# Twenty-eight of thirty-two attention steps put into a hardware loop of seven passes

## The chip, the cores and the metric

The kernel runs on one core of a Trainium2 chip. The core has five engines that run at the same time, each with an instruction queue of its own: TensorE (PE in the profile; its weight loads are listed as PEld), VectorE (DVE), ScalarE (ACT), GpSimd (POOL) and SyncE (SP). They order themselves by semaphores. Data come from memory through 16 DMA engines, which work through what the queues hand them; nearly every load here is issued by SyncE. The metric is the device time of one execution in microseconds (us).

## What is computed

A conditioned block decodes one token for each of 4 batch entries (B = 4): a layer norm with a condition-dependent scale and shift, attention over a cache of 4096 keys for 32 heads of width 128, and a small gated MLP. All tensors are bf16. The part that the change touches is the attention:

```python
q = (h @ wq).reshape(B, 1, 32, 128).transpose(0, 2, 1, 3)
scores = jnp.einsum('bhqd,bhkd->bhqk', q, k_cache) * 128 ** (-0.5)
p = softmax(scores, axis=-1)
o = jnp.einsum('bhqk,bhkd->bhqd', p, v_cache)
x = x + ga * (o.transpose(0, 2, 1, 3).reshape(B, 1, 4096) @ wo)
```

k_cache and v_cache have the shape (4, 32, 4096, 128), 134 MB each, and every element is used once.

## The kernel before

The attention is cut into 32 *quads*: quad i covers four heads, head group g = i // 4, of batch entry b = i % 4. The keys of one quad are 4 MB of contiguous memory and land in one SBUF tile of 128 partitions x 16384 elements (tag kt, two buffers that take turns); the values likewise (tag vt, two buffers, which the prologue uses first for the weights w_mod and wq).

The schedule is written by hand: each engine executes its instructions in the order in which the program emits them. The loop over the quads (line 429) is a Python loop, so all 32 steps are written out. Step i does this:

- SyncE: issue the load of K of quad i+1 (lines 92 and 431), at the first quad of a group also that group's slice wo_g of wo (line 436, 0.5 MB, two buffers), then the load of V of quad i (line 437). A load first waits until the last reader of its buffer is done.
- scores(i, half), lines 272 to 285, for the two halves of the keys: VectorE multiplies the K tile in place by the query (line 276, 128 x 8192 elements), and TensorE adds up the products over the head width with 16 matmuls against the identity (line 281) into a PSUM tile s_ps (two buffers). fold (line 290) reduces what is left over to S.
- softmax(i), lines 295 to 320: six short VectorE instructions, an exponential on ScalarE (line 311), then the probabilities P4 with a head mask (line 314; three buffers) and the row sums.
- values(i-1), lines 331 to 348: one matmul for the sum (zsum, line 327), 32 matmuls of P4 with V (line 341) into the PSUM tile big (two buffers), and a copy on ScalarE (line 347).
- diagonal(i-2) (line 354) and project(i-2) (lines 374 and 375) take the head outputs from there, divide and put them into oT; apply(i-2) (lines 381 to 408) multiplies a finished group's oT by wo_g into attn_ps, once for every four quads.

So work on a quad is spread over three steps: scores, one step later the values, one more step later the output. Quad 31 is special: its K comes in two pieces and its V in five, and behind them SyncE issues the weights that the end of the kernel needs (lines 440, 444, 446). The last V products are in values_last (line 363). Then comes the MLP, some 10 us of short instructions.

Small PSUM results (layer-norm sums, the outputs of the modulation, apply's transposition) use a PSUM tile with the tag small, one buffer.

Of the kernel before, what the change touches and what calls it, by code (L numbers as in the profile page):

```python
# [9 lines left out]
F32 = mybir.dt.float32  # L10
# [6 lines left out]
def kernel(  # L17
# [52 lines left out]
    def vslot(cols):  # L70
        return kvp.tile([P, cols], BF16, name="vt", bufs=2)

    wm = vslot(J * 6 * D)
# [3 lines left out]
    wq = vslot(J * G * GW)  # L77
# [3 lines left out]
    quads = [(g, b) for g in range(G) for b in range(B)]  # L81

    def kv_view(cache, i):
        g, b = quads[i]
        return cache[b, g * NH:(g + 1) * NH].rearrange("h (s n) d -> (h s) (n d)", s=R)

    def load(cache, i, tag, parts):
        t = kvp.tile([P, NT * DH], BF16, name=tag, bufs=2)
        a = 0
        for part in parts:  # L90
            b = a + NT * DH // part
            nc.sync.dma_start(out=t[:, a:b], in_=kv_view(cache, i)[:, a:b])  # L92
            a = b
        return t.rearrange("p (n d) -> p n d", d=DH)

    def load_k(i):
        return load(A_k_cache, i, "kt", (2, 2) if i == len(quads) - 1 else (1,))

    def load_v(i):
        return load(A_v_cache, i, "vt", (2, 4, 8, 16, 16) if i == len(quads) - 1 else (1,))  # L100

    NQ = len(quads)
# [23 lines left out]
    def keep_busy(n):  # L126

        if busy_ps[0] is None:
            busy_ps[0] = psum_s.tile([P, 4 * P], F32, name="big", bufs=2)
        for _ in range(n):  # L130
            nc.tensor.matmul(busy_ps[0], lhsT=ident, rhs=wide, start=True, stop=True)

    NB = 3
# [17 lines left out]
    def ln_stats(pool, psum, buf, ones, n, name, meanwhile=None):  # L151

        nc.vector.tensor_tensor(out=buf[:, 1], in0=buf[:, 0], in1=buf[:, 0], op=ALU.mult)
        ps = psum.tile([P, 2, n, B], F32, name="small", bufs=1)
# [38 lines left out]
    )  # L193

    def mod_part(oc):
        ps = psum_s.tile([P, J, B], F32, name="small", bufs=1)
        for jo in range(J):
            c0 = oc * D + (jo if oc < 2 else jo * P)
            cols = slice(c0, c0 + (P - 1) * J + 1, J) if oc < 2 else slice(c0, c0 + P)
            for j in range(J):  # L200
                nc.tensor.matmul(
                    ps[:, jo, :], lhsT=wm[:, j, cols],
                    rhs=sT[:, j, :], start=(j == 0), stop=(j == J - 1),
                )
        if oc in (1, 4):
            nc.vector.tensor_scalar_add(out=modT[:, oc], in0=ps, scalar1=1.0)
        else:
            nc.vector.tensor_copy(out=modT[:, oc], in_=ps)
# [13 lines left out]
    with tc.tile_pool(name="pre", bufs=1) as pre:  # L222
        xc_ps = psum_s.tile([P, J, 2 * B], F32, name="small", bufs=1)
# [5 lines left out]
        xt_ps = psum_s.tile([P, J, B], F32, name="big", bufs=2)  # L229
# [25 lines left out]
        wb_ps = psum_s.tile([P, 2], F32, name="small", bufs=1)  # L255
# [6 lines left out]
        for b in range(B):  # L262
            for g0 in range(0, G, 4):
                qp = psum_s.tile([P, 4, DH], F32, name="big", bufs=2)
                query(b, g0, 4, qp)
                nc.scalar.copy(out=qbc[:, b, g0:g0 + 4, :], in_=qp)


    with tc.tile_pool(name="psum_att", bufs=1, space=bass.MemoryType.PSUM) as psum:
        st = {}  # L270

        def scores(i, half):
            g, b = quads[i]
            kt = st["k", i][:, half * HT:(half + 1) * HT, :]
            q = qbc[:, b, g, :]
            nc.vector.tensor_tensor(  # L276
                out=kt, in0=kt, in1=q[:, None, :].to_broadcast([P, HT, DH]), op=ALU.mult,
            )
            ps = psum.tile([P, HT, DC], F32, name="s_ps", bufs=2)
            for cc in range(DH // DC):  # L280
                nc.tensor.matmul(  # L281
                    ps, lhsT=ident, rhs=kt[:, :, cc * DC:(cc + 1) * DC],
                    start=(cc == 0), stop=(cc == DH // DC - 1),
                )
            st["s", i, half] = ps

        def fold(i, half):
            if half == 0:
                st["S", i] = wk.tile([P, NT], F32, name="S", bufs=3)
            nc.vector.tensor_reduce(  # L290
                out=st["S", i][:, half * HT:(half + 1) * HT], in_=st.pop(("s", i, half)),
# [3 lines left out]
        def softmax(i):  # L295
            S = st.pop(("S", i))
            mx, P4 = mxs[i % NB], P4s[i % NB]
            nc.vector.tensor_reduce(out=mx[:, 0:1], in_=S, axis=AX.X, op=ALU.max)
            mT = wk.tile([P, R], F32, name="mT", bufs=2)
            nc.vector.transpose(out=mT, in_=mx)  # L300
            hm = wk.tile([P, 1], F32, name="hm", bufs=2)
            nc.vector.tensor_reduce(out=hm, in_=mT, axis=AX.X, op=ALU.max)
            hb = wk.tile([P, R], F32, name="hb", bufs=2)
# [3 lines left out]
            nm = wk.tile([P, R], F32, name="nm", bufs=2)  # L307
            nc.vector.transpose(out=nm, in_=hb)  # L308
            E = wk.tile([P, NT], F32, name="E", bufs=2)
            rs = wk.tile([P, 1], F32, name="rs", bufs=2)  # L310
# [7 lines left out]
            rs4 = wk.tile([P, NH], F32, name="rs4", bufs=3)  # L318
            nc.vector.tensor_scalar_mul(out=rs4, in0=mask4, scalar1=rs)
            st["rs4", i] = rs4  # L320

        def zsum(i):
            zo = psum.tile([P, 2, NH], F32, name="zo_ps", bufs=2)
            st["z", i], st["o", i] = zo[:, 0], zo[:, 1]
            if i == NQ - 1:
                st["z", i] = psum_s.tile([P, NH], F32, name="small", bufs=1)
            nc.tensor.matmul(
                st["z", i], lhsT=ones_f, rhs=st.pop(("rs4", i)), start=True, stop=True,
            )

        def values(i):


            P4 = P4s[i % NB]
            zsum(i)
            po = psum_s.tile([P, 4, DH], F32, name="big", bufs=2)
            NU = NT // 16
            for u in range(NU):
                for t in range(4):
                    n0 = 16 * u + 4 * t  # L340
                    nc.tensor.matmul(  # L341
                        po[32 * t:32 * t + 32], lhsT=P4[:, n0:n0 + 8, :],
                        rhs=st["v", i][:, n0:n0 + 4, :],
                        start=(u == 0), stop=(u == NU - 1), tile_position=(0, 32 * t),
                    )
            osb = wk.tile([P, 4, DH], F32, name="osb", bufs=2)
            nc.scalar.copy(out=osb, in_=po)  # L347
            st["osb", i] = osb

        def diagonal(i):  # L350

            osb = st.pop(("osb", i))
            for n in range(4):
                nc.tensor.matmul(  # L354
                    st["o", i], lhsT=osb[:, n, :], rhs=sel[:, NH * n:NH * n + NH],
                    start=(n == 0), stop=(n == 3),
                )

        def values_last(i):
            P4 = P4s[i % NB]  # L360
            zsum(i)
            for n in range(NT):
                nc.tensor.matmul(  # L363
                    st["o", i], lhsT=st["v", i][:, n, :], rhs=P4[:, n, :],
# [3 lines left out]
        def project(i):  # L368
            g, b = quads[i]
            if b == 0:  # L370
                st["oT", g] = wk.tile([P, NH, B], BF16, name="oT", bufs=2)
            oT = st["oT", g]
            rz = wk.tile([P, NH], F32, name="rz", bufs=2)
            nc.vector.reciprocal(out=rz, in_=st.pop(("z", i)))
            nc.vector.tensor_tensor(  # L375
                out=oT[:, :, b], in0=st.pop(("o", i)), in1=rz, op=ALU.mult,
            )
            if i == NQ - 1:
                apply(i)

        def apply(i):
            g, b = quads[i]
            if b == B - 1:
                oT = st.pop(("oT", g))
                if g < G - 1:
                    wo_g = st.pop(("wo", g))

                    pp = psum_s.tile([P, NH, B], F32, name="small", bufs=1)
                    for r in range(NH):
                        for hl in range(NH):  # L390
                            nc.tensor.matmul(
                                pp[hl * R:(hl + 1) * R, r, :], lhsT=ident[:, r::NH],
                                rhs=oT[:, hl, :], start=True, stop=True,
                                tile_position=(0, hl * R),
                            )
                    oT = wk.tile([P, NH, B], BF16, name="oP", bufs=2)
                    nc.vector.tensor_copy(out=oT, in_=pp)  # L397
                for hl in range(NH):
                    for jo in range(J):
                        nc.tensor.matmul(  # L400
                            attn_ps[:, jo, :],
                            lhsT=(wo_g[:, hl] if g < G - 1 else wo_l[hl // 2][:, hl % 2])[
                                :, jo * P:(jo + 1) * P],
                            rhs=oT[:, hl, :],
                            start=(g == 0 and hl == 0 and jo == 0),
                            stop=(g == G - 1 and hl == NH - 1),
                            skip_group_check=True,
                        )
# [18 lines left out]
        wo_l = [wk.tile([P, NH // 2, D], BF16, name=f"wo_l{a}", bufs=1) for a in range(2)]  # L427
        st["k", 0] = load_k(0)
        for i in range(NQ):
            if i + 1 < NQ:  # L430
                st["k", i + 1] = load_k(i + 1)
            if quads[i][1] == 0:
                g = quads[i][0]
                if g < G - 1:
                    st["wo", g] = wk.tile([P, NH, D], BF16, name="wo_g", bufs=2)
                    nc.sync.dma_start(out=st["wo", g], in_=wo_w[g])
            st["v", i] = load_v(i)
            if i == NQ - 1:
# [6 lines left out]
                for a, (j0, j1) in enumerate(JFS):  # L445
                    nc.sync.dma_start(out=wout[a], in_=wout_v[a])
            if i > 1:
# [3 lines left out]
            scores(i, 0)  # L451
            if i > 1:
                project(i - 2)
            scores(i, 1)
# [8 lines left out]
            if i > 1:  # L463
                apply(i - 2)
# [3 lines left out]
        project(NQ - 1)  # L468


    with tc.tile_pool(name="post", bufs=1) as post, \
# [67 lines left out]
        t_ps = psum_s.tile([J * B, P], F32, name="small", bufs=1)  # L539
# [36 lines left out]
```

## Time and profile before

| | |
|---|---|
| median of 3 runs | 667.62 us (667.53 to 667.81) |
| span of the profiled execution, first to last instruction | 665.5 us |
| read from memory | 282.73 MB, 425 GB/s over the span |
| longest busy engines | PE 415.7 us, DVE 402.6 us |
| K multiply, line 276 | 64 x 4.42 us |
| K sums on TensorE, line 281 | 1024 matmuls, 457 ns each in the mean |
| fold, line 290 | 64 x 0.69 us |
| K load, 4 MB, issue to landing | 26.0 us (median) |
| V load, 4 MB, issue to landing | 33.7 us (median) |
| SyncE's queue waiting for the multiply (line 276), for the K sums (line 281), for the V products (line 341) | 379.1, 139.5, 37.0 us |

The span and the runs' times are not the same thing: the profiled execution's own time, as the profile has it, is its span, and the runs' median lies 2.1 us above it, for what is done around the first and the last instruction.

The profile's views are read as follows. The page counts busy time of each engine, and shows it in 40 slices of the span as a digit for tenths. The DMA line is the share of the 16 DMA engines that is busy; q1 is SyncE's data queue, q8 and q14 bring instructions. The chain of waits is followed back from the last instruction: at each step it shows what released the instruction. SyncE's timeline lists the issue of each load. The trace also has a record for each DMA packet (start, length, bytes, queue) and for each landing: a load runs on 16 DMA engines, and each of them raises the load's semaphore when its part is in.

### The profile page before, as it was taken

The numbers are of one execution on the slowest core, as the hardware profiler recorded it, in microseconds if no ns is written. First come the engines' busy times: TensorE is split into PE (matmuls) and PEld (weight loads), VectorE is DVE, ScalarE is ACT, GpSimd is POOL, SyncE is SP. The second block draws the span as 40 slices with busy tenths as digits, with TensorE's granted clock in tenths as the row PEclk, the third lists the DMA queues.
The fourth block names the chain that finished last, engine by engine and source line by source line (L and its number), as shares of the span: only waits on it lengthen the run. The fifth ranks groups of instructions, "written<-read, shape, count | busy, mean of one in ns | idle before, by whom it ended". The sixth has DMA issues, their size and how long they took to land.

```text
span 665.5 us, 6939 instructions
## 1 busy us (share of the span) xinstructions
PE 415.7 (62%) x3024; PEld 204.6 (31%) x3024; DVE 402.6 (61%) x475; ACT 41.3 (6%) x115; POOL 4.7 (1%) x21
## 2 busy tenths in 40 slices
PE   2557776655677655676555477654657655657775
PEld 2223333222333322233222233232223322223334
DVE  2166776675556576547666456666555666655762
ACT  1200000000000000000000000000000000000002
POOL 2000000000000000000000000000000000000000
PEclk9977777668887667887667788676888766888795
DMA  9999999999999999999999999999999999999995
GB/s 379 439 425 427 437 439 424 429 438 434 427 428 441 428 428 434 435 426 434 433 436 424 436 435 430 423 439 435 428 431 435 433 430 432 437 426 435 428 417 236
DMA packets 12749, 283.17 MB, mean 426 GB/s; under 512 B 1448, under 2 KB 1968, under 8 KB 4016
## 3 DMA queue, kind: packets, MB, share of 16 engines
q1 hardware_dynamic: 12640, 282.73, 98.9%
q8 instruction: 23, 0.38, 0.2%
q14 instruction: 6, 0.05, 0.0%
q0 software_dynamic: 64, 0.00, 0.0%
q10 hardware_dynamic: 16, 0.01, 0.0%
HBM read 282.73 MB, written 0.00 MB: 425 GB/s over the span
## 4 chain that ended last, share of the span: by engine, by line
DMA 62%; PE 24%; DVE 12%; issue 0%; SPq 0%; ACT 0%; DVEq 0%
DMA kt<-in_A_k_cache_dram 58%; PE s_ps L281 24%; DVE kt L276 11%; DMA vt<-in_A_v_cache_dram 3%; DMA wout_437<-in_B_w_out_dram 1%; PE big L341 0%; DVE S L290 0%; ACT E L311 0%; SPq L92 0%; DVE P_1_109 L314 0%; DVE P_0_105 L314 0%; PE y_ps L522 0%; DVE nm L308 0%; DVE mT L300 0%; SPq L78 0%
## 5 line engine op out<-in xcount | busy, mean ns | idle before, releaser
L281 PE MATMUL s_ps<-kt,ident 128*128 128x512 bf16 x1024 | 293.5, 457 | 185.5 <-DVE kt L276 185.5
L276 DVE TENSOR_TENSOR kt<-kt,qbc 128x8192 bf16<-128x8192 bf16 x64 | 282.7, 4420 | 82.9 <-DMA kt<-in_A_k_cache_dram 82.9
L281 PEld LDWEIGHTS <-ident 128*128 128x128 bf16 x1024 | 116.4, 114 | 351.1 <-issue 229.8
L290 DVE TENSOR_REDUCE S<-s_ps 128x64 f32<-128x512 f32 x64 | 44.3, 692 | 125.5 <-PE s_ps L281 125.5
L354 PE MATMUL zo_ps<-sel,osb 128*128 128x4 f32 x248 | 33.2, 257 | 26.6 <-ACT osb L347 26.6
L311 ACT ACTIVATE E<-S,nm 128x128 f32<-128x128 f32 x32 | 12.8, 401 | 563.4 <-DVE nm L308 563.4
L354 PEld LDWEIGHTS zo_ps<-sel,osb 128*128 128x128 f32 x248 | 30.6, 194 | 38.4 <-ACT osb L347 38.4
L341 PE MATMUL big<-vt,P_0_105 128*32 128x512 bf16 x352 | 21.0, 380 | 1.5 <-DMA vt<-in_A_v_cache_dram 1.5
L341 PE MATMUL big<-vt,P_1_109 128*32 128x512 bf16 x320 | 19.1, 380 | 0.0
L341 PE MATMUL big<-vt,P_2_113 128*32 128x512 bf16 x320 | 19.1, 380 | 0.0
L347 ACT COPY osb<-big 128x512 f32<-128x512 f32 x31 | 17.6, 566 | 20.0 <-PE big L341 20.0
L215 PE MATMUL big<-vt,hbc 128*32 128x512 bf16 x128 | 9.6, 471 | 5.2 <-DMA vt<-in_A_wq_dram 5.2
L314 DVE TENSOR_TENSOR P_1_109<-E,mask_99 128x512 bf16<-128x512 f32 x11 | 7.6, 692 | 6.8 <-ACT E L311 6.8
L314 DVE TENSOR_TENSOR P_0_105<-E,mask_99 128x512 bf16<-128x512 f32 x11 | 7.6, 692 | 6.7 <-ACT E L311 6.7
L341 PEld LDWEIGHTS <-P_0_105 128*32 128x32 bf16 x352 | 8.4, 96 | 8.9 <-DMA vt<-in_A_v_cache_dram 1.6
L314 DVE TENSOR_TENSOR P_2_113<-E,mask_99 128x512 bf16<-128x512 f32 x10 | 6.9, 692 | 6.2 <-ACT E L311 6.2
L400 PE MATMUL attn_ps<-oP,wo_g 128*128 128x4 bf16 x112 | 3.8, 164 | 10.6 <-DVE oP L397 10.6
L341 PEld LDWEIGHTS <-P_1_109 128*32 128x32 bf16 x320 | 7.6, 96 | 6.7
L341 PEld LDWEIGHTS <-P_2_113 128*32 128x32 bf16 x320 | 7.6, 96 | 6.7
L375 DVE TENSOR_TENSOR oT<-zo_ps,rz 128x4 bf16<-128x4 f32 x32 | 5.4, 168 | 7.1 <-PE zo_ps L363 6.0
L215 PEld LDWEIGHTS <-hbc 128*32 128x32 bf16 x128 | 4.4, 114 | 10.3 <-issue 8.4
L308 DVE STREAM_TRANSPOSE nm<-hb 128x32 f32<-128x32 f32 x32 | 6.8, 212 | 1.1
(221 smaller groups left out, 131.1 us busy)
## 6 DMA issues: line engine op xcount, KB each, us to landing
kt<-in_A_k_cache_dram SPq DMA_DIRECT2D x31, 4096.0 KB, 26.0
vt<-in_A_v_cache_dram SPq DMA_DIRECT2D x31, 4096.0 KB, 33.7
vt<-in_A_wq_dram SPq DMA_DIRECT2D x1, 4096.0 KB, 20.4
kt<-in_A_k_cache_dram SPq DMA_DIRECT2D x2, 2048.0 KB, 24.8
wo_g<-in_A_wo_dram SPq DMA_DIRECT2D x7, 512.0 KB, 26.5
vt<-in_w_mod_dram SPq DMA_DIRECT2D x1, 3072.0 KB, 9.8
vt<-in_A_v_cache_dram SPq DMA_DIRECT2D x1, 2048.0 KB, 17.8
win_434<-in_B_w_in_dram SPq DMA_DIRECT2D x1, 1344.0 KB
```

The source lines that it names most:

```text
L215: nc.tensor.matmul(qp[hl * R:(hl + 1) * R, 0:n], lhsT=hbc[:, j, b, :], rhs=wv[:, g0:g0 + n, hl, :], start=(j == 0), stop=(j == J - 1), til ...
L276: nc.vector.tensor_tensor(out=kt, in0=kt, in1=q[:, None, :].to_broadcast([P, HT, DH]), op=ALU.mult,)
L281: nc.tensor.matmul(ps, lhsT=ident, rhs=kt[:, :, cc * DC:(cc + 1) * DC], start=(cc == 0), stop=(cc == DH // DC - 1),)
L290: nc.vector.tensor_reduce(out=st["S", i][:, half * HT:(half + 1) * HT], in_=st.pop(("s", i, half)), axis=AX.X, op=ALU.add,)
L308: nc.vector.transpose(out=nm, in_=hb)
L311: nc.scalar.activation(out=E, in_=S, func=AF.Exp, bias=nm[:, 0:1], scale=att_scale, accum_out=rs,)
L314: nc.vector.tensor_tensor(out=P4[:, 0:NT, :], in0=E[:, :, None].to_broadcast([P, NT, NH]), in1=mask4[:, None, :].to_broadcast([P, NT, NH]) ...
L341: nc.tensor.matmul(po[32 * t:32 * t + 32], lhsT=P4[:, n0:n0 + 8, :], rhs=st["v", i][:, n0:n0 + 4, :], start=(u == 0), stop=(u == NU - 1), ...
L347: nc.scalar.copy(out=osb, in_=po)
L354: nc.tensor.matmul(st["o", i], lhsT=osb[:, n, :], rhs=sel[:, NH * n:NH * n + NH], start=(n == 0), stop=(n == 3),)
L375: nc.vector.tensor_tensor(out=oT[:, :, b], in0=st.pop(("o", i)), in1=rz, op=ALU.mult,)
L400: nc.tensor.matmul(attn_ps[:, jo, :], lhsT=(wo_g[:, hl] if g < G - 1 else wo_l[hl // 2][:, hl % 2])[:, jo * P:(jo + 1) * P], rhs=oT[:, hl, :],
```

## The change

Quads 2 to 29 are no longer written out; they are four steps in a hardware loop of seven passes. Each engine runs the four steps and branches back. Steps 0, 1, 30 and 31 stay written out before and behind the loop. To make the four steps the same in each pass:

- every tile that was taken from a rotating pool becomes a fixed pair, picked by i % 2 (kt, vt, s_ps, zo_ps, S, E, rs, rs4, osb, big, P4, mx), or a single one (mT, hm, hb, nm, rz, oT, oP, wo_g). P4, mx, S and rs4 thereby go from three buffers to two, wo_g, oT and oP from two to one;
- the loads' memory addresses and the query's row are picked by the loop's counter k, a register;
- the load of wo_g moves from the first quad of a group, ahead of V, to the third, behind V, seven loads as before;
- attn_ps is zeroed by a matmul with zeros before the loop, instead of by the first product's start flag;
- the PSUM tile small is one fixed tile with views.

The keyword iteration_sync="reg_based" is the form of the loop: there is no barrier between passes. The loop has semaphores of its own, which are preset by one pass's counts before it, only ever grow while it runs, and are cleared behind it; a wait in the body compares with a register that each pass raises.

```diff
-    quads = [(g, b) for g in range(G) for b in range(B)]
-    def load_k(i):
-        return load(A_k_cache, i, "kt", (2, 2) if i == len(quads) - 1 else (1,))
-    def load_v(i):
-        return load(A_v_cache, i, "vt", (2, 4, 8, 16, 16) if i == len(quads) - 1 else (1,))
+    k_all = A_k_cache.rearrange("b (g h) (s n) d -> b g (h s) (n d)", h=NH, s=R)
+    v_all = A_v_cache.rearrange("b (g h) (s n) d -> b g (h s) (n d)", h=NH, s=R)
+    def load_k(i, g):
+        load(kt[i % 2], k_all[i % B, g], (2, 2) if i == NQ - 1 else (1,))
+    def load_v(i, g):
+        load(vt[i % 2], v_all[i % B, g], (2, 4, 8, 16, 16) if i == NQ - 1 else (1,))
...
-    NB = 3
+    NB = 2
...
-        for i in range(NQ):
+        def step(i, g1, g, g2):
             if i + 1 < NQ:
-                st["k", i + 1] = load_k(i + 1)
-            if quads[i][1] == 0:
-                g = quads[i][0]
-                if g < G - 1:
-                    st["wo", g] = wk.tile([P, NH, D], BF16, name="wo_g", bufs=2)
-                    nc.sync.dma_start(out=st["wo", g], in_=wo_w[g])
-            st["v", i] = load_v(i)
+                load_k(i + 1, g1)
+            load_v(i, g)
             if i == NQ - 1:
...
+            elif i >= 2 and i % B == 2 and g2 is not None:
+                nc.sync.dma_start(out=wo_g, in_=wo_w[g2])
             if i > 1:
                 diagonal(i - 2)
...
-            if i > 1:
-                apply(i - 2)
+            if i > 1 and (i - 2) % B == B - 1:
+                apply()
+        nc.tensor.matmul(
+            attn_ps.rearrange("p j b -> p (j b)"), lhsT=ident, rhs=wide[:, 0:J * B],
+            start=True, stop=False, skip_group_check=True,
+        )
+        load_k(0, 0)
+        step(0, 0, 0, None)
+        step(1, 0, 0, None)
+        with tc.For_i(0, G - 1, 1, iteration_sync="reg_based") as k:
+            step(2, k, k, k)
+            step(3, k + 1, k, None)
+            step(4, k + 1, k + 1, None)
+            step(5, k + 1, k + 1, None)
+        step(NQ - 2, G - 1, G - 1, None)
+        step(NQ - 1, G - 1, G - 1, None)
         diagonal(NQ - 2)
         project(NQ - 2)
         values_last(NQ - 1)
         project(NQ - 1)
+        product(oT, lambda hl: wo_l[hl // 2][:, hl % 2], True)
```

Inside a pass the order is therefore, for SyncE: K of step 3, V of step 2, wo_g; K of 4, V of 3; K of 5, V of 4; K of the next pass's step 2, V of 5: nine loads.

## The prediction

> **What bounds the kernel now.** I read the page's counts and slices first, then the chain that ended last, then SyncE's part of the timeline, then the records of single packets and landings.
>
> ```profile
> PE 415.7 (62%) x3024; PEld 204.6 (31%) x3024; DVE 402.6 (61%) x475; ACT 41.3 (6%) x115; POOL 4.7 (1%) x21
> DMA  9999999999999999999999999999999999999995
> q1 hardware_dynamic: 12640, 282.73, 98.9%
> q8 instruction: 23, 0.38, 0.2%
> ```
> No engine is busy for more than 62%, and the 16 DMA engines are busy in every slice but the last. 8064 of q1's packets are of 32 KB, and on one engine they follow each other every 1.2095 us: 16 x 32768 B / 1.2095 us = 433 GB/s, so 282.73 MB need 652 us. The last load lands on the 16 engines at 658.7 us in the mean and 660.89 on the last one. Loads are the bound.
>
> ```profile
> 588.48 25.58 DMA kt<-in_A_k_cache_dram
> 614.05 0.02 issue
> 614.08 4.44 DVE kt L276
> 618.51 0.04 issue
> 618.55 9.71 PE s_ps L281 x32
> ```
> This piece of the chain of waits shows a loop of buffers: a K load is issued, lands 25.6 us later, is multiplied and summed, and that frees the buffer. But a 4 MB load takes 9.7 us on the engines; the other 16 us are spent behind loads already queued. When K of quad 30 is issued at 588.48, K of 29 lands at 594.7 and V of 28 at 604.3: the engines have **15.9 us of work in hand**. Whatever delays an issue by less than that costs nothing.
>
> ```profile
> 608.38 0.80 SPq L92 DMA_DIRECT2D kt<-in_A_k_cache_dram  x2
> 610.35 22.14 SPq L92 DMA_DIRECT2D vt<-in_A_v_cache_dram  x6
> 632.54 0.43 SPq L440 DMA_DIRECT2D wo_l_438<-in_A_wo_dram  x1
> 633.54 0.37 SPq L440 DMA_DIRECT2D wo_l_439<-in_A_wo_dram  x1
> 643.21 0.37 SPq L444 DMA_DIRECT2D win_434<-in_B_w_in_dram  x1
> ```
> SyncE's queue at the end. The first weight load (L444) has no data to wait for and still goes out only at 643.21, when V of quad 30 lands; the waits of SyncE's queue give this as 13.7 us in two waits, "SPq L444 <- DMA vt". The landing semaphores that the DMA records name say why: there are eight, taken in turn, and V of 30 is the eighth load before L444. **A load waits until the one that had its semaphore before it has landed.** Eight back, that binds only here.
>
> **The change, part by part, on the path first.**
>
> Back edge. The loop body issues nine loads: four K, four V, one wo_g. With eight semaphores in turn, the ninth (V of step 5) takes the first one's (the K load that step 2 issues), and the next pass starts with that load again. Written out flat, the rotation simply went on; in a loop it is frozen. If each pass's first K waits for V of the pass before, which stands directly in front of it in the queue, the engines run dry once a pass. Price, from records: landing is told 0.45 us after the last packet (258.59 to 259.04 for one K load); SyncE's issue to the first packet took 1.00 us at the start (0.75 to 1.75) and 0.86 at the end (663.16 to 664.02), say 0.95; and the 16 engines do not end together, so the mean engine also idles until the last one is through: the last landing is 1.2 us behind the mean of the 16 at 110 us, 1.0 at 228, 2.5 at 614. Restarted together each 80 us, they drift little: I take 1.2. Sum **2.6 us** (bounds 1.7, for a drift of 0.24 as in the first load, 10.27 to 10.51, to 3.9 for one of 2.5). Six back edges: 15.6 us.
>
> Entry. The loop has semaphores of its own, which count up and are preset by one pass; so what a body instruction needs from before the loop must be awaited ahead of the first pass. SyncE's body loads overwrite the slots of K of 2 and V of 1, so it waits for both to land: another dry queue, 2.6 us, and a join of the engines, for which the nearest row is the one at the start of the program (first instruction at 0.00, SyncE's first load at 0.75). 3.35 us; bounds 0 and 5.
>
> Exit. The loop's semaphores are cleared behind it, so everything that counts on them, V of 29 too, must have landed before any engine goes on. What is late next is the tail. In the trace K of 30 is multiplied from 614.08, as soon as it lands; behind a join, only at T, the join's end. From the rows: first multiply to the last sum of quad 30 614.08 to 628.99 = 14.9; from quad 31's multiply (628.91) to its zsum 17.9, less the 0.9 us that rows of V of 30 cost there, so 17.0; 128 products with V (64 took 1.87 us) 3.75; from the last of them to the output's issue 653.40 to 663.16 = 9.76; to the end of the span 2.3. That is T + 47.7, whereas the loads alone would have ended about 5 us sooner: today's cover of the tail by V of 31 is gone.
>
> Costed at nothing: a register update and a separate wait at each wait, address arithmetic for nine loads (SyncE spends 0.33 us on an issue now, each pass is near 80 us), the query's row picked by a register, three buffers turned to two (P4, S, rs4), wo_g, oT and oP single. All lie inside the 15.9 us. In detail, a second P4 buffer is free once values(i-2) has run, which stands ahead of scores(i) on TensorE; wo_g is asked for behind V of step 2 and needs the 16 products of step 5 done, and behind it in SyncE's queue stands only a K load that is due 14 us later. The zeroing matmul runs while K of 0 is still in flight (chain: 1.64 to 31.2). [...] Bytes loaded are the same.
>
> Code pages are the other thing that the branch touches. q8's 23 packets of 16 KB come one per 256 TensorE instructions, take 0.93 us of one DMA engine, and the next is fetched about one page ahead. [...] The rows give bounds: a pass has 328 matmuls with as many weight loads, 2.6 pages, so it refetches three pages or none. TensorE's branch falls where it waits 5.2 to 6.3 us for the multiply anyway (idle before L281 at 223, 243 and 619 us); a fetch of 1 to 6 us is hidden, and 15.9 us stand behind that. So 0, or at the other end -15 x 0.93 / 16 = -0.9 us if the body stays resident.
>
> **Sum**, against the profiled span of 665.5 us; the runs' median of 667.62 is 2.1 us more, for what lies around it. V of 29 lands at 621.4 in the mean over the engines; + entry 3.35 + six edges 15.6 + drift at the exit 1.2 = 641.6; + join 0.75: T = 642.3; + 47.7 = 690.0; + 2.1 = **692 us**. With the bounds of a dry queue, and tail and joins at nothing or double, 680 to 702.
>
> **Rivals.**
> *Joins only.* The loop's semaphores are dealt so that a pass's first K does not wait for the V ahead of it. For it: a loop may have more than eight. Against: the flat program has eight and does wait. V of 29's last landing 621.4 + 3.35 + 2.2 (drift of a long stretch) = 627.0, T = 627.7, end 675.4 + 2.1 = 677.6; 672 if the tail stays covered. 0.25.
> *Nothing drains.* The rotation and the joins leave the 15.9 us in the queue; then bytes decide and the time stays at 667.6, within 0.2% (1.3 us, about what these runs can tell from no change). For it: the share of DMA time. [...] 0.08.
> *Faster.* Only one mechanism could do it: the body's code stays on the chip, so fewer pages disturb single DMA engines. 0.9 us less in the mean and the final drift of 2.15 us down to 1.2 gives 665.8. It decides only if all joins together cost under 0.5 us. 0.03.
> *Worse.* Loads wait for a landing in every quad, or the waits' register work passes the cover: 28 x 2.6 us gives 740, others fall between. 0.09.
>
> **How the numbers follow.** The forecast, one dry queue a pass, has 0.55. 673 to 701 holds it and the joins-only case; outside lie no change, faster, and worse, together 0.2. Slower by over 0.2%: 0.55 + 0.25 + 0.09 = 0.89; within 0.08; faster 0.03.
>
> **What would show it.** Right: gaps of 2 to 3 us in the DMA packets once each 80 us, each ending with a pass's first K load released by the landing of a V load; those K loads landing in some 11 us instead of 26; a gap before K of 31 and a tail in which the last V parts are in before quad 31's softmax. Joins only: two gaps. Wrong altogether: DMA at 433 GB/s through all slices. A busier DVE between K's landing and the last matmul of a quad, with loads issued late, would mean that the register work is what costs.

## The result, and the profile after

| | before | after |
|---|---|---|
| median of runs | 667.62 us | 689.19 us (688.37 to 690.97) |
| ratio | | 1.0327, 95% interval 1.0312 to 1.0342 |
| span of the profiled execution | 665.5 us | 686.5 us |

The change makes the kernel 3.3% slower. The forecast was 692 us, for one dry queue a pass. The GB/s line of the page before, and four lines of the page after, whose DMA line was all nines but for the last slice before:

```profile
GB/s 379 439 425 427 437 439 424 429 438 434 427 428 441 428 428 434 435 426 434 433 436 424 436 435 430 423 439 435 428 431 435 433 430 432 437 426 435 428 417 236
```

```profile
DMA  9999999989999899998999899998999989999896
GB/s 379 437 432 430 427 427 428 437 336 429 445 437 430 359 433 430 428 430 365 428 430 439 384 407 449 428 428 367 416 439 433 441 347 439 445 426 430 337 417 238
q1 hardware_dynamic: 12640, 282.73, 96.6%
q8 instruction: 8, 0.13, 0.1%
```

The same bytes in as many packets, but the GB/s line now dips to 336 to 384 at even distances: seven dips, six for the back edges and one for the exit. Between them the rate is about that of before, mostly 426 to 445. The engines' sums hardly moved (PE 415.7 to 409.7 us, DVE 402.6 to 404.6). SyncE's timeline from one V load to the next K load before, then SyncE's timeline around the second back edge after, and the lines of its queue's waits that changed (one before, two after):

```profile
115.70 0.33 SPq L92 DMA_DIRECT2D vt<-in_A_v_cache_dram  x1
133.62 0.33 SPq L92 DMA_DIRECT2D kt<-in_A_k_cache_dram  x1
```

```profile
196.49 0.33 SPq L88 DMA_DIRECT2D kt<-in_A_k_cache_dram  x1
198.79 0.33 SPq L88 DMA_DIRECT2D vt<-in_A_v_cache_dram  x1
231.02 0.33 SPq L88 DMA_DIRECT2D kt<-in_A_k_cache_dram  x1
231.71 0.33 SPq L88 DMA_DIRECT2D vt<-in_A_v_cache_dram  x1
232.31 0.33 SPq L436 DMA_DIRECT2D wo_g<-in_A_wo_dram  x1
```

```profile
SPq L92 <- DMA vt<-in_A_v_cache_dram: 13.3, 1, 13.3
```

```profile
SPq L88 <- DMA vt<-in_A_v_cache_dram: 95.0, 6, 16.2
SPq L463 <- DMA vt<-in_A_v_cache_dram: 29.3, 1, 29.3
```

After the V load of 198.79, 32 us go by without an issue, where the kernel before has 15 to 20; then three come within 1.3 us. Six waits, one for each back edge, are for a V load: SyncE's next instruction is a pass's first K load. The records give the semaphores: in the loop, eight (122 to 129) in turn; the pass's last V raises 122, and the next pass's first K goes out behind that landing and raises 122 again (at the second edge V lands at 230.81, the K is issued at 231.02). L463 is the loop's own line: at the exit, SyncE waits 29.3 us for the landing of a V load.

What a dry queue looks like, by stretches: the gap at the first back edge, and a stretch behind the second one, whose gap ends at 231.98 (columns: start and end, length, busy time of PE, PEld, DVE, ACT, POOL with counts, granted clock, DMA share, GB/s):

```profile
148.70:150.30 1.60, 1.60 (x9) 0.72 (x8) 0.63 (x1) 0.00 (x0) 0.00 (x0) 1.00 0.00 0
238.00:262.00 24.00, 13.99 (x82) 6.87 (x82) 12.86 (x15) 0.99 (x4) 0.00 (x0) 0.72 1.00 433
```

For 1.6 us no packet moves at all while TensorE works on; from 6 us behind the gap on, the DMA engines are full again. In the packet records each of the six edges has 1.61 us without a packet, of which 0.63 is from the last packet's end to SyncE's issue and 0.98 from there to the first packet; with the engines that ended earlier, the mean engine is idle for 2.0 to 2.9 us (16 engines' time around the gap, less what the packets took).

One caution in reading: in the page's chain after, "PE 3%; DVE 3%; ACT 0%; issue 0%; DVEq 0%; ACTq 0%" is all that is left. The first piece in it is the multiply at 639.89, behind the loop's exit; of the loop, whose waits are against registers, it has nothing. The DMA line and the queue's waits had to do.

### The profile page after: what moved, and what is told of

Same layout as the page of the kernel before. It is cut to its first block, busy times and chain, and to the rows that moved or that the text cites. A ratio compares the mean times of both kernels' runs of the same rounds, so it can differ in the third digit from the quotient of the medians.

```text
span 686.5 us, 7844 instructions
## 1 busy us (share of the span) xinstructions
PE 409.7 (60%) x3024; PEld 204.3 (30%) x3025; DVE 404.6 (59%) x475; ACT 41.1 (6%) x115; POOL 4.1 (1%) x19
## 5 line engine op out<-in xcount | busy, mean ns | idle before, releaser
L311 PE MATMUL s_ps<-kt,ident 128*128 128x512 bf16 x1024 | 287.0, 450 | 201.5 <-DVE kt L306 164.3
L354 PE MATMUL big<-vt,P 128*32 128x512 bf16 x992 | 59.2, 380 | 0.0
L335 DVE TENSOR_TENSOR P<-E,mask 128x512 bf16<-128x512 f32 x32 | 22.2, 692 | 20.7 <-ACT E L332 20.7
L354 PEld LDWEIGHTS <-P 128*32 128x32 bf16 x992 | 23.7, 96 | 20.8
L342 PEld LDWEIGHTS zo_ps<-rs,ones_f 128*128 128x128 f32 x62 | 11.8, 190 | 4.5
L325 DVE TENSOR_REDUCE mx<-S 128x1 f32<-128x128 f32 x32 | 9.1, 286 | 1.2
L342 PE MATMUL zo_ps<-rs,ones_f 128*128 128x4 f32 x62 | 8.7, 211 | 0.0
L326 DVE STREAM_TRANSPOSE mT<-mx 128x32 f32<-128x32 f32 x32 | 6.8, 211 | 1.1
L339 DVE TENSOR_SCALAR rs<-mask,rs 128x4 f32<-128x4 f32 x32 | 7.1, 223 | 0.0
L384 PEld LDWEIGHTS <-wo_g 128*128 128x128 bf16 x112 | 3.8, 96 | 10.5 <-issue 10.4
```

Source lines behind the costliest of these rows:

```text
L311: nc.tensor.matmul(s_ps[half], lhsT=ident, rhs=kh[:, :, cc * DC:(cc + 1) * DC], start=(cc == 0), stop=(cc == DH // DC - 1),)
L335: nc.vector.tensor_tensor(out=P4[:, 0:NT, :], in0=E[:, :, None].to_broadcast([P, NT, NH]), in1=mask4[:, None, :].to_broadcast([P, NT, NH]) ...
L342: nc.tensor.matmul(z_last if i == NQ - 1 else zo_ps[i % 2][:, 0], lhsT=ones_f, rhs=rs4_t[i % 2], start=True, stop=True,)
L354: nc.tensor.matmul(po[32 * t:32 * t + 32], lhsT=P4[:, n0:n0 + 8, :], rhs=v[:, n0:n0 + 4, :], start=(u == 0), stop=(u == NU - 1), tile_posi ...
L384: nc.tensor.matmul(attn_ps[:, jo, :], lhsT=w(hl)[:, jo * P:(jo + 1) * P], rhs=o[:, hl, :], start=False, stop=(last and hl == NH - 1), skip ...
```

## The experiments

All times are compared with runs of the kernel before on the same chip (667.31 to 667.37). "Gaps" are stretches in the packet records in which no DMA engine has a packet, before the last load's end. The runs were made on three chips, on which the kernel before differs by 0.06 us.

### The change without the loop

```diff
-        with tc.For_i(0, G - 1, 1, iteration_sync="reg_based") as k:
+
+        def one_pass(k):
...
+        for k in range(G - 1):
+            one_pass(k)
```

> The changed kernel with its loop written out: fixed buffers, wo_g behind V, zeroing matmul all as in the change, but a Python loop. Theory (the loop's frozen rotation of landing semaphores costs the time): 667.6 us within 1.5, no stretch without DMA packets before the end, 20 or more instruction packets on q8. Rival (two buffers instead of three, or wo_g's single buffer and new place, cost it): 675 or more, with loads issued late.

Measured 670.61 us, ratio 1.0047 (1.0031 to 1.0064). No gap, 23 instruction packets; the DMA line is again all nines but for the last slice:

```profile
DMA  9999999999999999999999999999999999999995
```

So the loop carries 18.6 of the 21.6 us. But 3 us are left that neither the theory (667.6 within 1.5) nor the rival as stated had: the loads are issued as far ahead as before (a V load lands 33.7 us after its issue in both, in the median), yet a 32 KB packet follows the last one after 1213.1 ns in the mean and no longer after 1209.4. Over some 504 such packets on each engine this is 1.8 us; smaller packets are longer too (those of 4 KB take 162.5 ns instead of 159.5).

### Ten loads a pass

```diff
-                nc.sync.dma_start(out=wo_g, in_=wo_w[g2])
+                for a in range(2):
+                    rs = slice(a * NH // 2, (a + 1) * NH // 2)
+                    nc.sync.dma_start(out=wo_g[:, rs], in_=wo_w[g2][:, rs])
```

> The loop as in the change, but wo_g is loaded in two halves: ten loads a pass, one issue more. Theory: the pass's first K now takes the semaphore of the last K, not of the last V, so 9.7 us of V stay in hand and the six gaps at the back edges (some 2.3 us of idle DMA and 0.6 us of slow first packets each, 17 us together) go; only the gap at the exit and the late tail stay: 672 us, 669 to 675. Rival (the branch, the register waits or a missing instruction page at the back edge cost it): 689, gaps unchanged.

Measured 673.44 us, ratio 1.0100 (1.0081 to 1.0119). One load more for each pass makes the kernel 15.8 us faster. The page and SyncE's timeline around the same back edge:

```profile
DMA  9999999999999999999999999999999999999796
```

```profile
196.52 0.33 SPq L88 DMA_DIRECT2D vt<-in_A_v_cache_dram  x1
219.10 0.33 SPq L88 DMA_DIRECT2D kt<-in_A_k_cache_dram  x1
228.81 0.33 SPq L88 DMA_DIRECT2D vt<-in_A_v_cache_dram  x1
229.41 0.93 SPq L438 DMA_DIRECT2D wo_g<-in_A_wo_dram  x2
```

The first K goes out at 219.10, when the K ahead of it has landed, with a V load still in hand; the V behind it waits for that V, 9.7 us later, with a K in hand. One gap is left, at the exit. The loop with its branches and register waits is as it was, so they are not what the back edge cost.

### Four passes in the loop, three written out

> The loop as in the change, nine loads a pass, but only four passes; the last three are written out behind it. Theory: three back edges instead of six, 3 x 2.9 = 8.7 us less, and the exit's gap (3.0 us idle, 0.7 us slow packets) lies in the middle, where nothing is late behind it: 678 to 681. Rival (exit and tail are most of the 21.6 us): 687 or more if the exit costs as much in the middle, 671 or less if the tail behind it does.

```diff
-        with tc.For_i(0, G - 1, 1, iteration_sync="reg_based") as k:
+
+        def one_pass(k):
...
+        with tc.For_i(0, 4, 1, iteration_sync="reg_based") as k:
+            one_pass(k)
+        for k in range(4, G - 1):
+            one_pass(k)
```

Measured 682.44 us, ratio 1.0223 (1.0206 to 1.0240): 6.8 us less for three edges fewer, which is 1.4 us less of a gain than the least expected (681). Four gaps: three of 1.6 us and one of 2.1 at the exit, now at 395 us. The dose goes the right way; 16 instead of 8 instruction packets on q8 can have given back a part (by an estimate 8 x 0.93 / 16 = 0.5 us), the rest is open.

### A full join at each back edge

```diff
-        with tc.For_i(0, G - 1, 1, iteration_sync="reg_based") as k:
+        with tc.For_i(0, G - 1, 1, iteration_sync="barrier") as k:
```

> The loop as in the change with a full join of all engines at each back edge, in place of waits that count up. Theory: each edge then drains the queue like the exit does, 3.0 to 4.5 us instead of 2.9, so 689 + 6 x (0.5 to 1.6) = 692 to 699. Rival (a join also holds back the sums of the K that has landed, so that the engines fall behind): 705 or more.

Measured 697.98 us, ratio 1.0462 (1.0445 to 1.0480). The six gaps are 3.2 us long in place of 1.6. A join of all engines is thus 1.5 us an edge dearer than the frozen rotation (8.8 us over six), and of the same kind: a queue that runs dry. The rival's 705 us, with engines that fall behind, did not come.

### Seventeen loads a pass

```diff
-        load(kt[i % 2], k_all[i % B, g], (2, 2) if i == NQ - 1 else (1,))
+        load(kt[i % 2], k_all[i % B, g], (2, 2))
-        load(vt[i % 2], v_all[i % B, g], (2, 4, 8, 16, 16) if i == NQ - 1 else (1,))
+        load(vt[i % 2], v_all[i % B, g], (2, 4, 8, 16, 16) if i == NQ - 1 else (2, 2))
```

> The changed kernel with every K and V load of the loop issued in two halves: seventeen loads a pass. Packets of 16 KB follow each other every 607 ns, so half loads alone cost some 2.5 to 3 us. Theory (eight semaphores in turn): the seventeenth load, the second half of the last V, again has the semaphore of the pass's first load, so the six gaps stay: 691 to 694. Rival (ten loads helped because there was one more load in hand, or because wo_g was smaller): the gaps are gone here too, 675 to 678.

Measured 692.82 us, ratio 1.0377 (1.0361 to 1.0393). The page shows the dips of the change again:

```profile
DMA  9999999989999899998999899998999989999796
```

Nine loads run dry, ten don't, seventeen do, with gaps of 1.6 us. Of the counts tried, those with a remainder of one by eight run dry; the number and the size of the loads do not decide.

### The exit in the middle

Ten loads a pass and four passes in the loop, the two diffs above together.

> Ten loads a pass (wo_g in halves) and four passes in the loop, the last three written out: the exit's dry queue alone, with half a kernel behind it to cover late work. Against ten loads and seven passes (673.4) it tells what the late tail behind the exit costs. Theory with a late tail of about 5 us, as the prediction had it: 669. Theory that the tail's lateness is mostly covered: 672 to 674 (nothing for the tail, some 0.6 us more for instruction pages of the part written out).

Measured 674.89 us, ratio 1.0107 (1.0092 to 1.0123), above both expectations. Moving the exit away from the end gains nothing. The median lies 1.4 us over that of ten loads and seven passes, but the runs of the two overlap (673.63 to 675.71 here, 672.99 to 675.66 there), so a loss is not shown. The tail is thus not late behind the exit by the 5 us that the prediction charged; with that, 669 was expected.

### The place of the buffers

The 3 us without the loop pointed to the DMA writes. In the kernel before, the first of the four K and V tiles begins at byte 56064 of each partition's row, 219 x 256, and the others 32768 bytes apart. With one P4 (1056 bytes) and one mx (128) less in front of them they begin at 54880, which is 96 bytes past a multiple of 256. Four kernels, each with a constant made longer and nothing else. First the written-out kernel and then the loop, with 160 bytes more:

```diff
-    eps = consts.tile([P, 1], F32, name="eps")
+    eps = consts.tile([P, 41], F32, name="eps")
     nc.vector.memset(eps, LN_EPS)
+    eps = eps[:, 0:1]
```

> The written-out kernel with fixed buffers (670.6), with a constant made 160 bytes longer, so that the K and V buffers begin at multiples of 256 bytes in each partition's row as in the kernel before (they began at 32 bytes past a multiple of 64). Theory (the buffers' place makes each 32 KB packet 4 ns longer, 1213.3 ns from packet to packet instead of 1209.4): 668.5, and 1209.4 again. Rival (the packets are longer for another reason, wo_g's place in the queue or the chip): 670.6, 1213.

Measured 667.63 us, ratio 1.0005 (0.9996 to 1.0014): all 3 us are gone, more than expected, and the period is 1209.4 ns again.

> The changed kernel (689.2) with the same 160 bytes more. Theory (place of the buffers): 1.3 us less, since the packets that follow a dry queue within some 30 us already run at 1209 ns: 687 to 688.3. Rival (place has no effect): 689.2. The six gaps stay in both.

Measured 687.11 us, ratio 1.0297 (1.0282 to 1.0311): 2.1 us less. The six gaps stay, at 1.4 to 1.5 us.

The written-out kernel with 25 columns (96 bytes more, 192 past a multiple of 256):

> The written-out kernel with fixed buffers, and the constant 96 bytes longer instead of 160: K and V buffers begin at multiples of 64 bytes, but 192 past a multiple of 256. If 64 is what counts: 667.6 and 1209.4 ns from packet to packet, as with 160 bytes more. [...]

Measured 670.80 us, ratio 1.0051 (1.0036 to 1.0065), 1213.5 ns. A multiple of 64 is no help.

The kernel before with 9 columns (32 bytes more):

> The kernel before, nothing changed but a constant that is 32 bytes longer, so that its K and V buffers begin 32 bytes past a multiple of 256. Theory (the buffers' place alone): 670 to 671, 1213 ns from packet to packet. Rival (the fixed buffers of the change were needed for the cost too): 667.4.

Measured 671.19 us, 0.2 above what was expected, ratio 1.0056 (1.0043 to 1.0069), 1214.4 ns. The shift alone does it, without any part of the change. The same stretch of the kernel before, of the written-out kernel at 96 bytes past, of the one at a multiple of 256, and of the kernel before shifted by 32, one line from each:

```profile
100.00:600.00 500.00, 310.40 (x2049) 149.66 (x2050) 313.34 (x335) 24.16 (x75) 0.00 (x0) 0.76 1.00 432
```

```profile
100.00:600.00 500.00, 308.14 (x2042) 148.77 (x2043) 311.03 (x332) 24.12 (x75) 0.00 (x0) 0.76 1.00 430
```

```profile
100.00:600.00 500.00, 310.48 (x2052) 149.50 (x2052) 313.37 (x336) 24.15 (x75) 0.00 (x0) 0.76 1.00 432
```

```profile
100.00:600.00 500.00, 308.37 (x2049) 148.93 (x2049) 310.08 (x333) 24.13 (x75) 0.00 (x0) 0.76 1.00 430
```

The DMA share is 1.00 in all four; the GB/s differ, 430 against 432. A full DMA line does not say that the packets are as short as they can be.

With the buffers at a multiple of 256 bytes the packets follow each other every 1209.4 ns, at 32, 96 or 192 past one every 1213.1 to 1214.4: 4 to 5 ns in 1209 for these 32 KB rows. Only the place in SBUF moved, so it is the side that is written. That 256 is the least multiple that does it is not shown, since one of 128 was not tried. What the 4 to 5 ns go to is not shown either: behind a gap the same loads run at 1209 ns for a while (last section).

### Both repairs

> The changed kernel with both repairs, ten loads a pass and buffers at multiples of 256 bytes. Theory (the two costs add up; what is left is the exit's dry queue, less the instruction pages that the loop no longer fetches): 673.4 less 2.5 to 3.0 = 670.4 to 671. If the exit were hidden by the pages saved: 667.6. One gap, at the exit.

Measured 671.01 us, ratio 1.0051 (1.0037 to 1.0065). One gap of 2.0 us, at the exit.

> As with ten loads and aligned buffers, but wo_g in four pieces, twelve loads a pass: the pass's first K now takes the semaphore of a K load two quads back, and more stays in hand. Theory (ten loads already leave enough in hand): the same as ten within 1 us. Rival (with ten loads the queue still runs thin): 1 to 3 us faster than ten.

Measured 670.74 us, ratio 1.0057 (1.0043 to 1.0071): the same. Ten loads leave enough in hand.

So the loop can be had for some 3.4 to 3.7 us, but no version here beats the kernel before. Of what it could save, the runs show only the instruction pages, 15 x 0.93 / 16 = 0.9 us by an estimate, and one gap, at the exit, is left.

## Why the prediction was right

The forecast's mechanism held, and so did its size: 692 against 689.2. That it came within 3 us is in part luck: the entry and the exit were charged 5.2 us too much, and 2.1 us of another cause were not seen.

| term | predicted | shown by | measured |
|---|---|---|---|
| six back edges | 15.6 us, 2.6 each | aligned buffers, nine against ten loads: 687.11 - 671.01 | 16.1, 2.7 each |
| entry | 3.35 | gap records: none before the first edge | 0 |
| exit and tail (what is left of the 692) | some 5.5 | ten loads, aligned, against before: 671.01 - 667.36 | 3.65, with the pages saved and all that the loop's instructions cost in it |
| place of the buffers | not seen | 689.19 - 687.11 | 2.1 |
| instruction pages | 0 to -0.9 | q8 packets 23 to 8 | in the 3.65 |

*Back edge.* Right in cause and price. The price was built from 0.45 for the landing to be told, 0.95 to the first packet and 1.2 for engines that end apart. Measured: 1.61 without any packet (0.63 and 0.98), and 2.0 to 2.9 with the engines that end apart. Something was missing and something was too large. The first packets behind a gap are slow, see below. And the engines drift less than the assumed 1.2: at the first edge the last landing is 1.05 us behind the mean of the 16, at the other five 0.14 to 0.37. From 97 us to the exit no instruction page of TensorE is fetched; that this is the reason was not tried. Two of the signs named ahead came as well: a gap each 82 us, and the K loads behind it land in 12.0 to 12.2 us instead of 26.0.

*Entry.* The term that failed. "SyncE's body loads overwrite the slots of K of 2 and V of 1, so it waits for both to land" is not what it does: the loop's first K goes out at 63.76 us, against 62.14 before, while V of 1 was still on its way, until 68.95. At the entry SyncE waited 17.1 us for VectorE and not for landings; the kernel before issues at nearly the same time. The entry was covered by the 5.2 us of work in hand. A line of before and two of after:

```profile
62.14 0.33 SPq L92 DMA_DIRECT2D kt<-in_A_k_cache_dram  x1
```

```profile
63.76 0.35 SPq L88 DMA_DIRECT2D kt<-in_A_k_cache_dram  x1
```

```profile
SPq L88 <- DVEq L463: 17.1, 1, 17.1
```

*Exit.* Right that everything lands first: the loop's last V is in at 639.15, the loop's semaphores are cleared at 639.60 (EVENT_SEMAPHORE_RANGE_CLEAR on GpSimd), 639.91 is the first issue behind 605.96, and the multiply of quad 30 starts at 639.89, when TensorE's and VectorE's waits for the join end.

```profile
605.96 0.33 SPq L88 DMA_DIRECT2D vt<-in_A_v_cache_dram  x1
639.91 0.83 SPq L88 DMA_DIRECT2D kt<-in_A_k_cache_dram  x2
```

```profile
639.89 4.42 DVE L306 TENSOR_TENSOR kt<-kt,qbc 128x8192 bf16<-128x8192 bf16 x1 [12.79 <-PEq L577]
```

T was 639.89, predicted 642.3; from there to the end of the span took 46.6 us, predicted 47.7. But "the loads alone would have ended about 5 us sooner" was wrong: the last load's last packet is at 680.91 and the span ends 5.6 us later, where it was 4.9 before. The loads behind the join need nearly as long as the late engines do. The sign named for the late tail did not come either: the last V part lands at 672.55, while quad 31's softmax runs from 668.07. And with the exit in the middle nothing was gained.

*Costed at nothing.* This held for the loop's own instructions. VectorE executes 280 register operations (ALU_OP) and 77 fused ones more than before, TensorE 70 and 21, and with ten loads no gap is left at a back edge; what they cost, if anything, lies within the 3.65 us. It did not hold for the buffers: going from three P4 and mx to two was costed as a wait that is covered, which is true, and moved every tile behind them, which was not asked.

*Instruction pages.* No pass had to fetch its pages again. q8 fetches pages up to 97 us and then none until 640: TensorE's body of about 2.6 pages stayed on the chip for seven passes. Its branch takes 0.22 to 0.24 us at each of the six back edges (COMPARE_BRANCH records).

What stays open: how the 3.65 us of the exit divide between the gap, the engines' restart and the late tail, and whether an exit in the middle is dearer than one at the end, which the runs here don't tell apart.

## What to carry to other kernels

Count what rotates. What the flat program deals out in turn, here eight landing semaphores, was frozen by the loop; with nine loads a body, the first of a pass waited for the last of the pass before (95.0 us in six waits), while with ten it waited for the K ahead of that V (34.1 us in six). In a kernel that the DMA engines bound, look not at how busy the engines are, but at how much work the queue holds when the next load goes out: the loads in hand hid branches, register work and the entry, and nothing hid the one wait that emptied the queue. And when a change removes or adds a small tile, compare where the large ones begin (here it was worth 3.0 to 3.8 us).

## What the hardware showed that was not expected

- Writes of 32 KB rows into a partition that begin 32, 96 or 192 bytes past a multiple of 256 follow each other every 1213 to 1214 ns, at a multiple of 256 every 1209.4. Over this kernel, without a loop, it is 3.0 to 3.8 us.
- That cost is not there at once: behind each gap of the changed kernel the packets follow each other every 1209 to 1211 ns for some 30 us, about three 4 MB loads, and only then every 1213. Why was not tried.
- The first packet of each DMA engine behind a gap is slow: 1.55 to 2.14 us instead of 1.21 at the first gap, and over 1.5 us in 82 of 96 cases at the six. The kernel after has 89 packets of 32 KB that take over 1.5 us, the kernel before 24, which come singly. Spread over the engines this is 0.5 to 0.7 us for each gap.
